# Staging the w3 columns of a two-layer spectral MLP kernel in a tile of their own

## The chip, the cores and the metric

The kernel runs on one core of one Trainium2 chip. The metric is device time in microseconds (us), the median over runs; lower is better. The core has a matrix engine (TensorE, PE in the profile), a vector engine (DVE), an activation engine (ACT), GpSimd (POOL) and SyncE (SP), whose queue here issues all the DMAs. Each engine works through its own list of instructions in program order, and semaphores tie the lists together.

## What is computed

Two layers, each made of a Fourier mixing block A and an MLP block B, over x of 2048 rows by 512 columns:

```python
# A: mixing
a = einsum("bsd,ed->bse", x, hid_re);  b = einsum("bsd,ed->bse", x, hid_im)
y = einsum("ts,bse->bte", seq_re, a) - einsum("ts,bse->bte", seq_im, b)
# B: spatial-shift mixing, then a channel MLP
h  = gelu(layernorm(x) @ w1)                 # four column groups shifted by +1, -1, +2, -2 rows
x1 = x + shifted(h) @ w2
B  = x1 + gelu(layernorm(x1) @ w3) @ w4      # w3: 512 x 1376, w4: 1376 x 512
# twice:
x = x + A(layernorm(x));  x = x + B(layernorm(x))
```

All is float32. The kernel gets the accuracy by splitting each operand into a high part (a cast to the matmul format, made on ACT) and a low part (operand minus high part, made on DVE), and by three matmuls for each product: high by high, high by low, low by high (`mm3`, lines 280 to 283).

## The kernel before

The rows are worked on in four chunks of 512. `by_pairs` (line 753) does block B. First it goes through w1 and w2 for all four chunks (`shifted` and `mixed`). Small jobs beside these products have written-down places: `D(slot, ...)` and `A(slot, ...)` put a job at slot 8c + 0..7 of chunk c, before (D) or after (A) the vector work of that slot. These jobs make, of chunks 0 and 1 (in layer 1 later also 2 and 3), the normalised input z3 of the second MLP. It goes through DRAM (`z3d`) to be turned, and comes back as blocks `b11`, `b21`, `b12`, `b22` and their Winograd sums `bt1` to `bt4`.

Then the product with w3 is done for two chunks at once, by a Winograd scheme of seven products instead of eight. Layer 1 does both pairs of chunks in this way, layer 0 one pair, and then chunks 2 and 3 by the plain `mlp` (line 699) with a stream of weights through `raw` and `ring`.

The loop over pairs of w3 column tiles (line 1048; p = 0 to 4) takes seven w3 units of one buffer `w3b[p % 2]`. Units 4, 5, 0 and 6 are tiles of w3 as they are; four sums (`w3_sums`, line 871) make units 0 to 3. In layer 0 the kernel makes highs (`w3_highs`), lows (`w3_lows`) and stores the whole 1792 KB buffer to DRAM (`w3_keep`, line 886), from where layer 1 loads it ready-made.

One turn of the loop has this order on PE, each `prod` being six matmuls:

```python
prod(b1, w, 4, "11"); copy u       # ACT takes b1 out of PSUM
prod(b6, w, 1, "t2"); v = u + b6   # add(): DVE, line 446
prod(b5, w, 0, "t1"); x = v + b5
prod(b2, w, 5, "21"); u = u + b2;  gelu and split of u
prod(b7, w, 2, "t3"); v = v + b7;  y = v + b5;  gelu of y
w4_part x 2                        # 12 matmuls each, of the turn before (one in turn 0)
prod(b4, w, 6, "t4"); v = v + b4;  gelu and split of v
prod(b3, w, 3, "22"); x = x + b3;  gelu of x
```

The seven results go round in four PSUM banks, so that a product begins only when the result four products earlier has been taken out.

In the kernel before, `w3_load(n)` puts the raw tiles of column pair n straight into the low half of `w3b[n % 2]` (lines 868 and 869). The loop issues it at the end of turn p for pair p + 2 (line 1092), when the buffer's last product has been issued. The sums, splits and stores for pair p + 1 and the same for two w4 tiles stand in a list `prep`; `one()` (line 997) takes the next entry from `prep`, or when it is empty from the background list `bg`. `bg` holds the z3 work of chunks 2 and 3 (`finish`: two sums each on DVE and the normalisation on ACT; `turn3`: transposes on DVE; `turn_out`: four stores of 256 KB).

`w4_load`, `w4_high` and `w4_low` (lines 838 to 855) do for tiles of w4 what the above does for w3: load, cast, low part and store to DRAM. There are six buffers `w4r`; each load waits until PE is done with its buffer. After the loop come two more `w4_part` for the pair's first chunk and eleven for the second, with one `one()` after each of the eleven. Then chunks 2 and 3 begin with `mlp`, whose first weight pieces are loaded by `more` (line 1104) and split by `ahead` from `bg`.

Of the kernel before, what the change touches and what calls it, by code (L numbers as in the profile page):

```python
# [19 lines left out]
CH = 512  # L20
# [13 lines left out]
RAW = 4  # L34
# [9 lines left out]
def spectral_mlp_kernel(ctx: ExitStack, tc: tile.TileContext, x, ws, hs, w1, w2, w34, out):  # L44
# [32 lines left out]
    base = -(-nc.sbuf_base // 32) * 32  # L77
    EXT = RNG + RING * 4 * CH
    RAWS = EXT + 6 * D
    nc.alloc_sbuf_tensor("arena", [P, RAWS + RAW * 2 * CH], F32)  # L80

    def at(name, word, *shape, dtype=F32R):
        return nc.alloc_sbuf_tensor_at(name, [P, *shape], dtype, offset=base + 4 * word).ap()
# [27 lines left out]
    w3b, w3bf = zip(*(both(f"w3b{i}", RNG + 8 * CH + i * 28 * P, 2, 7, 2 * P) for i in range(2)))  # L111
    h4 = [at(f"h4{i}", RR + 8 * CH + i * 2 * CH, 2, CH) for i in range(4)]
    hc = at("hc", W12, NF, CH, dtype=F32)
    w4_at = [ZW + i * 2 * CH for i in range(4)] + [W12 + NF * CH + i * 2 * CH for i in range(2)]
    w4r, w4rf = zip(*(both(f"w4r{i}", word, 2, CH) for i, word in enumerate(w4_at)))
    scratch = [at(f"scr{i}", RNG + w * 4 * CH, KD, CH, dtype=F32) for i, w in enumerate((2, 3, 0))]
# [636 lines left out]
    def by_pairs(layer, zs, xin, dst):  # L753
# [107 lines left out]
        def w3_load(n):  # L861
            if n >= n_pairs * (NF // 2):
                return
            if layer:
                nc.sync.dma_start(w3b[n % 2].bitcast(F32), w3d[n % (NF // 2)])
                return
            lo = w3bf[n % 2][:, 1]
            nc.sync.dma_start(lo[:, 4:6], w34[2 * n][:, 0].rearrange("p (u w) -> p u w", u=2))
            nc.sync.dma_start(lo[:, 0:7:6], w34[2 * n + 1][:, 0].rearrange("p (u w) -> p u w", u=2))

        def w3_sums(n):

            lo = w3bf[n % 2][:, 1]
            add(lo[:, 2], lo[:, 4], lo[:, 0], ALU.subtract)
            add(lo[:, 0], lo[:, 0], lo[:, 6])
            add(lo[:, 1], lo[:, 0], lo[:, 4], ALU.subtract)
            add(lo[:, 3], lo[:, 5], lo[:, 1], ALU.subtract)

        def w3_highs(n, a, b):
            nc.scalar.copy(w3b[n % 2][:, 0, a:b], w3bf[n % 2][:, 1, a:b])  # L880

        def w3_lows(n, a, b):
            w = w3b[n % 2]
            nc.vector.tensor_tensor(w[:, 1, a:b], w3bf[n % 2][:, 1, a:b], w[:, 0, a:b].bitcast(F32), op=ALU.subtract)  # L884

        def w3_keep(n):
            nc.sync.dma_start(w3d[n], w3b[n % 2].bitcast(F32))
# [75 lines left out]
        D(25, u_stats(2, 2))  # L963

        A(26, lambda: w3_load(0))
        A(28, lambda: w3_load(1), *[w4_load] * 4)
        if layer == 0:
            A(30, lambda: w4_high(0), lambda: w4_high(1))
            D(31, lambda: w4_low(0), lambda: w4_low(1), lambda: w3_sums(0))
            A(31, lambda: w3_highs(0, 0, 7))  # L970
        for c in range(NC):
            tmps[:] = extra[4:6]
            count["tmp"] = 0
# [18 lines left out]
            for q in range(TC):  # L992
                nc.vector.tensor_tensor(xt(c * TC + q), acc[q], xt(c * TC + q), op=ALU.add)

        bg, prep = [], []

        def one():
            if prep:
                prep.pop(0)()
            elif bg:  # L1000
                bg.pop(0)()

        for pair in range(n_pairs):
# [2 lines left out]
            acc2 = [bk[(1 + i) % 4] for i in range(4)]  # L1006
            if pair == 0:
                bg += [finish(2, 0), finish(2, 2), turn3(turned, 2, 0, 1), turn3(turned, 2, 2, 3)]
                bg += [lambda: turn_out(turned, z3d[2]), u_stats(3, 0), u_stats(3, 2), finish(3, 0), finish(3, 2)]
                bg += [turn3(turned, 3, 0, 1), turn3(turned, 3, 2, 3), lambda: turn_out(turned, z3d[3])]  # L1010
            tmps[:] = gs
            if layer == 0:
                w3_lows(0, 0, 4)
                w3_lows(0, 4, 7)
            s = w4_use()
            for i, names in enumerate((("11", "21"), ("12", "22"))):
                for d in range(KD):
# [13 lines left out]

            def w_prep(p):

                todo = []
                if p == 0:
                    todo.append(lambda: w3_keep(0))
                if p + 1 < NF // 2:
                    todo.append(lambda: (w3_sums(p + 1), w3_highs(p + 1, 0, 4)))
                    todo.append(lambda: (w4_high(2 * p + 2), w3_highs(p + 1, 4, 7)))
                    todo.append(lambda: (w3_lows(p + 1, 0, 4), w4_high(2 * p + 3)))  # L1040
                    todo.append(lambda: (w3_lows(p + 1, 4, 7), w3_keep(p + 1)))
                    todo.append(lambda: (w4_low(2 * p + 2), w4_low(2 * p + 3)))
                else:
                    todo.append(lambda: (w4_high(NF - 1), w4_high(NF)))
                    todo.append(lambda: (w4_low(NF - 1), w4_low(NF)))
                return todo

            for p in range(NF // 2):
                if layer == 0:
                    prep += w_prep(p)  # L1050
                u, v, x, y = sets[p % 2]
                w = w3b[(5 * pair + p) % 2]
                b1, b6, b5, b2, b7, b4, b3 = (bk[(2 + 7 * p + i) % 4] for i in range(7))
                prod(b1, w, 4, "11")
                nc.scalar.copy(u, b1)
                if layer == 0:
                    one()
                prod(b6, w, 1, "t2")
                add(v, u, b6)
                prod(b5, w, 0, "t1")  # L1060
                one()
                add(x, v, b5)
                prod(b2, w, 5, "21")
                add(u, u, b2)
                gelu_split(h4[2 * (p % 2)], u, act)
                if layer == 0:
                    one()
                prod(b7, w, 2, "t3")
                add(v, v, b7)
                add(y, v, b5)  # L1070
                gelu(hc[:, 2 * p + 1], y)
                one()
                if p == 0:
                    w4_part(acc1, fs[0], h4[2], None if layer else one)
                    w4_load()
                else:
                    for i in range(2):
                        w4_part(acc1, 2 * p - 2 + i, h4[2 * ((p - 1) % 2) + i], None if layer else one)
                        w4_load()
                        one()  # L1080
# [6 lines left out]
                if layer == 0:  # L1087
                    one()
                prod(b3, w, 3, "22")
                add(x, x, b3)  # L1090
                gelu(hc[:, 2 * p], x)
                w3_load(5 * pair + p + 2)
                one()

            if layer and pair == 0:
# [3 lines left out]
                bg += [sum_of("t1", "12", "11"), sum_of("t2", "22", "t1"), sum_of("t3", "22", "12"), sum_of("t4", "21", "t2")]  # L1099
                bg += [parts(b) for b in ("11", "21", "12", "22", "t2", "t1", "t3", "t4")]  # L1100
            if layer == 0:
                nothing = lambda: None

                def more():
                    state.update(limit=w_items[1], load=len(pieces))
                    issue_dma()

                bg += [nothing, lambda: rt_in(2), more, nothing, nothing]
                bg += [lambda: rt_split(2, ((0, 2),)), lambda: rt_split(2, ((2, 4),)), lambda: ahead(1), lambda: ahead(1), lambda: ahead(1)]
            for i in range(2):  # L1110
                w4_part(acc1, NF - 3 + i, h4[i])
                w4_load()
# [12 lines left out]
            if last:  # L1125
                ss = [w4_use(), w4_use()]
                for q in range(TC):
                    v = slice(q * P, (q + 1) * P)
                    for k, s in zip((NF - 2, NF - 1), ss):
                        h = h4[(2 + k) % 4]  # L1130
                        mm3(acc2[q], h[:, 0, v], h[:, 1, v], s[:, 0], s[:, 1], False, k == NF - 1)
                    j = c2 * TC + q
                    nc.vector.tensor_tensor(xt(j), acc2[q], xt(j), op=ALU.add)
                    rows(xs[j // 2][:, j % 2 : j % 2 + 1], dst, j, 1, False)
            else:
                drain(c2, acc2)
                for j in range(c2 * TC, c2 * TC + TC, 2):
                    rows(xs[j // 2], dst, j, 2, False)
                while bg or prep:
                    one()  # L1140

    for layer in range(LAYERS):
# [148 lines left out]
        tmps[:] = singles  # L1291
        for c in (2, 3):
            for t in mlp(c, acc4, mm4):
                if c == 2 and t == 0:
                    rt_in(3)
                if c == 2 and t in (9, 10):
                    rt_split(3, ((2 * t - 18, 2 * t - 16),))
                if c == 3 and t == 1:
                    for j in range(2 * TC, 3 * TC, 2):
                        rows(xs[j // 2], x2d, j, 2, False)  # L1300
                n = STEPS * (c - 2) + t - 6
                if n >= 0:
                    if n == 0:
                        tmps[:] = [tmp[:, 4], tmp[:, 5]]
                    for k in range(6):
                        for step, f in enumerate(xp_stages):
                            if n == FIRST[k] + step:
                                f(k)
# [55 lines left out]
```

## Time and profile before

| | |
|---|---|
| runs | 1497.39, 1495.9, 1496.81 us; median 1496.81 |
| the profiled execution | 1495.02 us, of which 1493.2 us are the span from the first to the last instruction |
| busy share of the span | PE 98%, DVE 75%, ACT 48%, POOL 6% |
| DMA | 277.17 MB, mean 186 GB/s; HBM read 231.21 MB, written 44.83 MB |
| mean granted TensorE clock | 0.994 |

A row of a profile names the line of the kernel, the engine, the operation, and the tiles as output<-inputs, with buffer numbers left out: `rest` are the tiles u, v, x and y of the loop, `psa` and `psd` PSUM banks, `in_w` the raw weights in DRAM. In a row of a timeline the first number is the start in us, the second the duration, and what stands in brackets at the end is the idle time of the engine just before and who ended it. SPq is the DMA queue of SP: its row tells when a DMA is issued and how long issuing takes, and a separate row "DMA to landing" how long it takes from issue until the data have landed. A row of waits gives who waited at which line for whom, the sum in us, how often, and the longest. Matmuls overlap: one lasts about 0.39 us and the next begins after some 0.23.

### The profile page before, as it was taken

The numbers are of one execution on the slowest core, as the hardware profiler recorded it, in microseconds if no ns is written. First come the engines' busy times: TensorE is split into PE (matmuls) and PEld (weight loads), VectorE is DVE, ScalarE is ACT, GpSimd is POOL, SyncE is SP. The second block draws the span as 40 slices with busy tenths as digits, with TensorE's granted clock in tenths as the row PEclk, the third lists the DMA queues.
The fourth block names the chain that finished last, engine by engine and source line by source line (L and its number), as shares of the span: only waits on it lengthen the run. The fifth ranks groups of instructions, "written<-read, shape, count | busy, mean of one in ns | idle before, by whom it ended". The sixth has DMA issues, their size and how long they took to land.

```text
span 1493.2 us, 17313 instructions
## 1 busy us (share of the span) xinstructions
PE 1461.2 (98%) x6374; PEld 1193.8 (80%) x6374; DVE 1122.5 (75%) x1553; ACT 713.9 (48%) x947; POOL 85.6 (6%) x111
## 2 busy tenths in 40 slices
PE   9999999999999977999999999999999999999998
PEld 7888888888878755788787888888888888888887
DVE  6876987988778865555989889979978688646443
ACT  5563454544566633333646444544545566333231
POOL 2100000000001000000100000000000010000000
PEclk9999999999999999999999999999999999999999
DMA  6326556566446554761434566455575358668434
GB/s 232 135 90 207 197 184 223 172 206 243 158 131 183 194 207 159 270 232 62 140 134 156 172 209 204 163 199 209 165 257 184 127 152 299 198 217 309 157 134 155
DMA packets 111220, 277.17 MB, mean 186 GB/s; under 512 B 8480, under 2 KB 38432, under 8 KB 109216
## 3 DMA queue, kind: packets, MB, share of 16 engines
q1 hardware_dynamic: 111136, 276.07, 55.0%
q8 instruction: 50, 0.82, 0.2%
q14 instruction: 34, 0.28, 0.1%
HBM read 231.21 MB, written 44.83 MB: 185 GB/s over the span
## 4 chain that ended last, share of the span: by engine, by line
PE 81%; DVE 11%; DMA 3%; ACT 2%; issue 1%; SPq 1%; POOL 0%; DVEq 0%; ACTq 0%
PE psd L281 9%; PE psd L283 9%; PE psd L282 9%; PE psa L281 7%; PE psa L283 7%; PE psa L282 7%; PE psc L283 6%; PE psc L281 6%; PE psc L282 6%; PE psb L283 5%; PE psb L281 5%; PE psb L282 5%; DVE ring L244 3%; DMA raw<-in_ws 2%; DVE w3b L884 1%
## 5 line engine op out<-in xcount | busy, mean ns | idle before, releaser
L228 ACT CAST ring<-raw 128x1024 fp32r<-128x1024 f32 (+1 forms) x153 | 156.2, 1029 | 117.9 <-PE psd L283 49.3
L244 DVE TENSOR_TENSOR ring<-raw,ring 128x1024 fp32r<-128x1024 f32 (+1 forms) x153 | 181.6, 1191 | 27.9 <-ACT ring L228 27.5
L282 PE MATMUL psd<-ring,rr 128*128 128x512 f32 x208 | 80.9, 389 | 0.0
L281 PE MATMUL psd<-ring,rr 128*128 128x512 f32 x208 | 80.9, 389 | 0.0
L283 PE MATMUL psd<-ring,rr 128*128 128x512 f32 x208 | 80.9, 389 | 0.0
L645 DVE TENSOR_TENSOR h<-tmp,h 128x512 fp32r<-128x512 f32 x53 | 36.7, 692 | 49.4 <-ACT h L644 47.6
L321 POOL TENSOR_TENSOR rs<-ve,mhalf 128x4 f32<-128x4 f32 x16 | 27.8, 1738 | 611.7 <-DVE nm L320 611.7
L300 POOL TENSOR_TENSOR rs<-ve,mhalf 128x2 f32<-128x2 f32 (+1 forms) x33 | 32.8, 993 | 448.6 <-DVE nb L299 439.0
L329 ACT ACTIVATE tmp<-xs,nb,rs 128x512 f32<-128x512 f32 x58 | 44.7, 808 | 18.7 <-POOL nb L301 18.7
L235 ACT CAST ring<-ring2f 128x1024 fp32r<-128x1024 f32 x28 | 29.6, 1057 | 43.5 <-DVE ring2f L234 43.5
L281 PE MATMUL psc<-ring,ay 128*128 128x512 f32 x128 | 49.9, 390 | 0.3 <-ACT rr11f L471 0.3
L282 PE MATMUL psc<-ring,ay 128*128 128x512 f32 x128 | 49.9, 390 | 0.2 <-DVE ring L244 0.2
L283 PE MATMUL psc<-ring,ay 128*128 128x512 f32 x128 | 49.8, 389 | 0.0
L281 PE MATMUL psb<-ring,ay 128*128 128x512 f32 x128 | 49.8, 389 | 0.0
L282 PE MATMUL psb<-ring,ay 128*128 128x512 f32 x128 | 49.8, 389 | 0.0
L283 PE MATMUL psb<-ring,ay 128*128 128x512 f32 x128 | 49.8, 389 | 0.0
L244 DVE TENSOR_TENSOR ring<-ring1f,ring 128x1024 fp32r<-128x1024 f32 (+1 forms) x50 | 49.1, 983 | 0.5 <-ACT ring L235 0.3
L244 DVE TENSOR_TENSOR ring<-ring3f,ring 128x1024 fp32r<-128x1024 f32 (+1 forms) x50 | 49.1, 983 | 0.2
L235 ACT CAST ring<-ring0f 128x1024 fp32r<-128x1024 f32 x28 | 29.6, 1057 | 41.1 <-DVE ring0f L234 41.1
L282 PE MATMUL psa<-ring,ay 128*128 128x512 f32 x126 | 49.0, 389 | 0.0
L283 PE MATMUL psa<-ring,ay 128*128 128x512 f32 x126 | 49.0, 389 | 0.0
L281 PE MATMUL psa<-ring,ay 128*128 128x512 f32 x126 | 49.0, 389 | 0.0
(474 smaller groups left out, 4377.2 us busy)
## 6 DMA issues: line engine op xcount, KB each, us to landing
raw<-in_ws SPq DMA_DIRECT2D x183, 512.0 KB, 4.8
raw<-in_hs SPq DMA_DIRECT2D x56, 512.0 KB, 3.5
w4r<-w4d SPq DMA_DIRECT2D x55, 512.0 KB, 3.7
w3b<-w3d SPq DMA_DIRECT2D x10, 1792.0 KB, 7.2
raw<-in_w SPq DMA_DIRECT2D x26, 512.0 KB, 3.6
w3d<-w3b SPq DMA_DIRECT2D x5, 1792.0 KB, 5.7
x1d<-tmp SPq DMA_DIRECT2D x12, 512.0 KB, 6.8
xs<-x1d SPq DMA_DIRECT2D x12, 512.0 KB, 6.6
```

The lines of the kernel that those rows point to most:

```text
L228: nc.scalar.copy(dest[:, a:b, 0], r[0][:, a:b])
L235: nc.scalar.copy(dest[:, :, 0], lo)
L244: nc.vector.tensor_tensor(lo, src, hi.bitcast(F32), op=ALU.subtract)
L281: nc.tensor.matmul(o, lh, rh, start=first, stop=False)
L282: nc.tensor.matmul(o, lh, rl, start=False, stop=False)
L283: nc.tensor.matmul(o, ll, rh, start=False, stop=last)
L300: nc.gpsimd.tensor_tensor(rs[:, :n], ve[:, :n], mhalf[:, 0, :n], op=ALU.pow)
L321: nc.gpsimd.tensor_tensor(rs, ve, mhalf[:, :, :2], op=ALU.pow)
L329: nc.scalar.activation(o, s, AF.Identity, bias=mr[2], scale=mr[1])
L645: nc.vector.tensor_tensor(dst[:, 1], g, dst[:, 0].bitcast(F32), op=ALU.subtract)
L884: nc.vector.tensor_tensor(w[:, 1, a:b], w3bf[n % 2][:, 1, a:b], w[:, 0, a:b].bitcast(F32), op=ALU.subtract)
```

## The change

- A new tile `staged` (1024 words per partition) lies behind the arena; the DMA scratch, which nothing in the kernel uses, gets smaller in its place.
- In layer 0 `w3_load(n)` loads both raw tiles of column pair n into `staged` by one DMA. `w3_sums`, `w3_highs` and `w3_lows` read units 4, 5 and 6 from there, and write the buffer `w3b` only with results. Highs and lows come in up to three pieces: the sums (units 0 to 3), units 4 and 5, unit 6.
- The load of pair n + 1 is issued right behind the store of pair n, when the lows of pair n have read `staged`. Pair 0 is loaded where it was, pair 1 behind the first store.
- The list `prep` becomes a table of fixed points: after the first product (0), before the sum of the third (1), after the fourth (2), after the fifth (3), in the middle of the first `w4_part` (4) and of the second (5).
- Ahead of the loop, part of pair 0's splits and its sums move to slots 29 to 31, and the lows of the first two w4 tiles move from slot 31 to behind the last sum of `mixed`.
- In layer 0 the z3 work of chunk 3 moves from the loop to the background jobs behind it (with a scratch tile in place of the part of `hc`), ahead of `more`; `rt_in(2)` comes right behind the loop, `rt_in(3)` one step later in `mlp`.
- In layer 1, turn 0 has one `one()` more, and the second `w3_load` stands behind four `w4_load`.

```diff
-            lo = w3bf[n % 2][:, 1]
-            nc.sync.dma_start(lo[:, 4:6], w34[2 * n][:, 0].rearrange("p (u w) -> p u w", u=2))
-            nc.sync.dma_start(lo[:, 0:7:6], w34[2 * n + 1][:, 0].rearrange("p (u w) -> p u w", u=2))
+            nc.sync.dma_start(staged.rearrange("p f k w -> p f (k w)"), w34[2 * n : 2 * n + 2, :, 0].rearrange("f p w -> p f w"))
...
+        def w3_sums(n, half):
+            lo, (a, b) = w3bf[n % 2][:, 1], (staged[:, i] for i in range(2))
+            if half == 0:
+                add(lo[:, 2], a[:, 0], b[:, 0], ALU.subtract)
+                add(lo[:, 0], b[:, 0], b[:, 1])
+            else:
+                add(lo[:, 1], lo[:, 0], a[:, 0], ALU.subtract)
+                add(lo[:, 3], a[:, 1], lo[:, 1], ALU.subtract)
+
+        def w3_of(n):
+            return (slice(0, 4), w3bf[n % 2][:, 1, 0:4]), (slice(4, 6), staged[:, 0]), (slice(6, 7), staged[:, 1, 1:2])
...
-        A(28, lambda: w3_load(1), *[w4_load] * 4)
+        A(28, *[w4_load] * 4)
         if layer == 0:
+            A(29, lambda: w3_highs(0, 1, 2))
+            D(30, lambda: w3_lows(0, 1, 2), lambda: w3_sums(0, 0))
             A(30, lambda: w4_high(0), lambda: w4_high(1))
-            D(31, lambda: w4_low(0), lambda: w4_low(1), lambda: w3_sums(0))
-            A(31, lambda: w3_highs(0, 0, 7))
+            D(31, lambda: w3_sums(0, 1))
+            A(31, lambda: w3_highs(0, 0))
+        else:
+            A(28, lambda: w3_load(1))
...
             if layer == 0:
-                w3_lows(0, 0, 4)
-                w3_lows(0, 4, 7)
+                w4_low(0)
+                w4_low(1)
+                w3_lows(0, 0)
+                w3_keep(0)
+                w3_load(1)
...
+                n, i = p + 1, 2 * p + 2
...
+                return {
+                    0: [lambda: w3_sums(n, 0), lambda: w3_highs(n, 1, 2)],
+                    1: [lambda: w3_sums(n, 1), lambda: w3_highs(n, 0)],
+                    2: [w4_highs],
+                    3: [lambda: w3_lows(n, 0)],
+                    4: [lambda: w3_lows(n, 1, 2), lambda: w3_keep(n), lambda: w3_load(n + 1)],
+                    5: [w4_lows],
+                }
...
-                w3_load(5 * pair + p + 2)
+                if layer:
+                    w3_load(5 * pair + p + 2)
...
-                bg += [nothing, lambda: rt_in(2), more, nothing, nothing]
-                bg += [lambda: rt_split(2, ((0, 2),)), lambda: rt_split(2, ((2, 4),)), lambda: ahead(1), lambda: ahead(1), lambda: ahead(1)]
+                rt_in(2)
+                bg += z3_last(scratch[0])
+                bg += [lambda: (more(), rt_split(2, ((0, 2),))), lambda: rt_split(2, ((2, 4),)), *[lambda: ahead(1)] * 3]
```

`z3_last(t)` is the list of chunk 3's jobs: two `u_stats`, two `finish`, one `turn3`, and a second `turn3` with the `turn_out`.

More of the change, by code (lines that the diff above doesn't have):

```diff
@@ L79, in spectral_mlp_kernel @@
     RAWS = EXT + 6 * D
-    nc.alloc_sbuf_tensor("arena", [P, RAWS + RAW * 2 * CH], F32)
+    STG = RAWS + RAW * 2 * CH
+    nc.alloc_sbuf_tensor("arena", [P, STG + 2 * CH], F32)
     def at(name, word, *shape, dtype=F32R):
@@ L113, in spectral_mlp_kernel @@
     hc = at("hc", W12, NF, CH, dtype=F32)
+    staged = at("staged", STG, 2, 2, 2 * P, dtype=F32)
     w4_at = [ZW + i * 2 * CH for i in range(4)] + [W12 + NF * CH + i * 2 * CH for i in range(2)]
@@ L866, in w3_load, with w3_highs, w3_lows @@
                 return
-            lo = w3bf[n % 2][:, 1]
[L868 to L882, printed above, removed]
+            nc.sync.dma_start(staged.rearrange("p f k w -> p f (k w)"), w34[2 * n : 2 * n + 2, :, 0].rearrange("f p w -> p f w"))
[9 more added lines that the diff above has]
+            return (slice(0, 4), w3bf[n % 2][:, 1, 0:4]), (slice(4, 6), staged[:, 0]), (slice(6, 7), staged[:, 1, 1:2])
+        def w3_highs(n, *which):
+            for i in which:
+                units, src = w3_of(n)[i]
+                nc.scalar.copy(w3b[n % 2][:, 0, units], src)
+        def w3_lows(n, *which):
             w = w3b[n % 2]
-            nc.vector.tensor_tensor(w[:, 1, a:b], w3bf[n % 2][:, 1, a:b], w[:, 0, a:b].bitcast(F32), op=ALU.subtract)
+            for i in which:
+                units, src = w3_of(n)[i]
+                nc.vector.tensor_tensor(w[:, 1, units], src, w[:, 0, units].bitcast(F32), op=ALU.subtract)
         def w3_keep(n):
@@ L993, in drain, with at_point @@
                 nc.vector.tensor_tensor(xt(c * TC + q), acc[q], xt(c * TC + q), op=ALU.add)
-        bg, prep = [], []
+        bg, prep = [], {}
+        def at_point(i):
+            for f in prep.pop(i, ()):
+                f()
         def one():
-            if prep:
-                prep.pop(0)()
-            elif bg:
+            if bg:
                 bg.pop(0)()
@@ L1008, in by_pairs @@
                 bg += [finish(2, 0), finish(2, 2), turn3(turned, 2, 0, 1), turn3(turned, 2, 2, 3)]
-                bg += [lambda: turn_out(turned, z3d[2]), u_stats(3, 0), u_stats(3, 2), finish(3, 0), finish(3, 2)]
-                bg += [turn3(turned, 3, 0, 1), turn3(turned, 3, 2, 3), lambda: turn_out(turned, z3d[3])]
+                bg += [lambda: turn_out(turned, z3d[2])]
+                z3_last = lambda t: [
+                    *(u_stats(3, 0), u_stats(3, 2), finish(3, 0), finish(3, 2)),
+                    *(turn3(t, 3, 0, 1), lambda: (turn3(t, 3, 2, 3)(), turn_out(t, z3d[3]))),
+                ]
+                if layer:
+                    bg += z3_last(turned)
             tmps[:] = gs
             if layer == 0:
-                w3_lows(0, 0, 4)
-                w3_lows(0, 4, 7)
+                w4_low(0)
[3 more added lines that the diff above has]
+                w3_load(1)
             s = w4_use()
@@ L1032, in w_prep @@
             def w_prep(p):
[L1034 to L1046, printed above, removed]
+                n, i = p + 1, 2 * p + 2
+                w4_lows = lambda: (w4_low(i), w4_low(i + 1))
+                w4_highs = lambda: (w4_high(i), w4_high(i + 1))
+                if n == NF // 2:
+                    return {1: [w4_highs], 5: [w4_lows]}
+                return {
[6 more added lines that the diff above has]
+                }
             for p in range(NF // 2):
-                if layer == 0:
-                    prep += w_prep(p)
+                prep = {} if layer else w_prep(p)
                 u, v, x, y = sets[p % 2]
@@ L1055, in by_pairs @@
                 nc.scalar.copy(u, b1)
-                if layer == 0:
-                    one()
+                at_point(0)
                 prod(b6, w, 1, "t2")
@@ L1060, in by_pairs @@
                 prod(b5, w, 0, "t1")
-                one()
+                if layer:
+                    one()
+                at_point(1)
                 add(x, v, b5)
@@ L1065, in by_pairs @@
                 gelu_split(h4[2 * (p % 2)], u, act)
-                if layer == 0:
-                    one()
+                at_point(2)
                 prod(b7, w, 2, "t3")
@@ L1071, in by_pairs @@
                 gelu(hc[:, 2 * p + 1], y)
-                one()
-                if p == 0:
-                    w4_part(acc1, fs[0], h4[2], None if layer else one)
-                    w4_load()
[L1076 to L1080, printed above, removed]
+                if layer:
+                    one()
+                at_point(3)
+                tiles = [(fs[0], h4[2])] if p == 0 else [(2 * p - 2 + i, h4[2 * ((p - 1) % 2) + i]) for i in range(2)]
+                for i, (f, h) in enumerate(tiles):
+                    w4_part(acc1, f, h, lambda: at_point(4 + i))
+                    w4_load()
+                    one()
+                at_point(4)
+                at_point(5)
                 if p == NF // 2 - 1:
@@ L1086, in by_pairs @@
                 gelu_split(h4[2 * (p % 2) + 1], v, act)
-                if layer == 0:
-                    one()
                 prod(b3, w, 3, "22")
@@ L1091, in by_pairs @@
                 gelu(hc[:, 2 * p], x)
-                w3_load(5 * pair + p + 2)
+                if layer:
+                    w3_load(5 * pair + p + 2)
                 one()
@@ L1101, in by_pairs @@
             if layer == 0:
-                nothing = lambda: None
                 def more():
@@ L1138, in by_pairs @@
                     rows(xs[j // 2], dst, j, 2, False)
-                while bg or prep:
+                while bg:
                     one()
@@ L1293, in spectral_mlp_kernel @@
             for t in mlp(c, acc4, mm4):
-                if c == 2 and t == 0:
+                if c == 2 and t == 1:
                     rt_in(3)
@@ L1352 @@
     arrays = {f"in_{k}": np.ascontiguousarray(v) for k, v in arrays.items()}
-    nc = bacc.Bacc("TRN2", target_bir_lowering=False, num_devices=1, dynamic_dma_scratch_size=1024)
+    nc = bacc.Bacc("TRN2", target_bir_lowering=False, num_devices=1, dynamic_dma_scratch_size=512)
     args = [
```

## Prediction

> **What bounds the kernel now.** I read the page first, then TensorE's waits, then the stage in which they lie, cut into the five turns of its loop, and last the queues of that stage in order of time.
>
> ```profile
> span 1493.2 us, 17313 instructions
> ```
> ```profile
> PE psa L281 <- DVE rest L446: 11.8, 5, 4.5
> PE psd L281 <- DVE rest L446: 8.9, 6, 3.2
> ```
>
> The columns are us in total, times, and the longest. TensorE (PE) waits little in the whole span, and nearly all of it (20.7 us) is for line 446, the vector sums that empty its banks. All eleven waits lie in layer 0's loop over pairs of w3 columns. Busy time by turn (p = 0 to 4; each ends where the next one's first product begins):
>
> ```profile
> 511.41:526.20 14.79, 13.12 (x55) 9.91 (x54) 10.97 (x19) 8.58 (x13) 0.00 (x0) 1.00 0.36 143
> 526.20:549.06 22.86, 17.57 (x67) 12.99 (x66) 14.36 (x24) 6.96 (x11) 0.00 (x0) 0.92 0.47 181
> 549.06:575.82 26.76, 18.84 (x67) 14.04 (x66) 16.33 (x34) 8.49 (x14) 2.04 (x4) 0.88 0.57 187
> 575.82:601.54 25.72, 18.44 (x67) 13.47 (x66) 13.71 (x23) 8.47 (x13) 0.00 (x0) 0.90 0.54 185
> 601.54:617.54 16.00, 16.00 (x68) 13.01 (x67) 8.82 (x14) 6.85 (x12) 0.00 (x0) 0.94 0.97 348
> ```
>
> After the length come PE, weight loads, DVE, ACT, POOL (busy us and count), then granted clock, DMA share and GB/s. A turn has 42 products of w3 and 24 of w4 (12 in the first), 318 in all. An undisturbed stretch of layer 1 gives the pace:
>
> ```profile
> 1178.00:1242.00 64.00, 64.00 (x283) 51.89 (x282) 52.39 (x106) 41.03 (x60) 9.54 (x16) 1.00 0.59 175
> ```
>
> About 281 of these 283 start inside, so 0.2276 us each: 66 take 15.0 us, 318 take 72.4. The loop takes 106.1, so 33.7 us are lost there, 2.3% of the span. No engine is full in turns 1 to 3 (DVE 14.36 of 22.86); it is a chain of waits. What starts it:
>
> ```profile
> DVE w3b0f L446 <- DMA w3b0f<-in_w: 14.2, 2, 8.8
> DVE w3b1f L446 <- DMA w3b1f<-in_w: 7.1, 1, 7.1
> ```
>
> DVE stands before its sums of w3 tiles until they have landed, 21.3 us in three waits, and behind it in its queue stand the sums that free PE's banks. The tiles are late because of where SyncE (SP) issues them:
>
> ```profile
> 547.22 0.33 SPq L887 DMA_DIRECT2D w3d<-w3b  x1
> 547.78 1.47 SPq L855 DMA_DIRECT2D w4d<-w4r  x2
> 549.37 1.16 SPq L844 DMA_DIRECT2D w4r2f<-in_w  x1
> 550.58 6.57 SPq L595 DMA_DIRECT2D z3d<-hc  x4
> 557.26 1.84 SPq L844 DMA_DIRECT2D w4r3f<-in_w  x1
> 559.20 1.40 SPq L868 DMA_DIRECT2D w3b1f<-in_w  x1
> 560.65 0.47 SPq L869 DMA_DIRECT2D w3b1f<-in_w  x1
> ```
> ```profile
> 564.54 1.80 DVE L446 TENSOR_TENSOR w3b1f<-w3b1f 128x256 f32<-128x256 f32 x4 [7.06 <-DMA w3b1f<-in_w]
> ```
>
> The load of column pair 3 comes last in that list, behind four stores of z3; DVE's sums follow its landing at once.
>
> **The change, part by part.**
>
> *The loop.* The load for n+1 now goes to its own tile right behind the store w3_keep(n), as soon as DVE has run the last lows of n. It no longer waits for PE or stands behind z3's stores. But there is one staging tile, so a circle remains: landing, DVE's work to the lows, store and load, landing. If it is longer than PE's 15.0 us it sets the turn. Its durations, from starts that follow each other without a gap:
>
> ```profile
> 503.71 0.68 DVE L686 TENSOR_TENSOR rest<-psd,rest 128x512 f32<-128x512 f32 x1
> 504.31 1.21 DVE L407 TENSOR_TENSOR bt<-bt4f,bt 128x1024 fp32r<-128x1024 f32 x1
> 505.45 0.68 DVE L854 TENSOR_TENSOR w4r<-w4r0f,w4r 128x512 fp32r<-128x512 f32 x1
> 506.05 0.68 DVE L854 TENSOR_TENSOR w4r<-w4r1f,w4r 128x512 fp32r<-128x512 f32 x1
> 506.65 1.79 DVE L446 TENSOR_TENSOR w3b0f<-w3b0f 128x256 f32<-128x256 f32 x4
> 508.36 0.68 DVE L686 TENSOR_TENSOR rest<-psa,rest 128x512 f32<-128x512 f32 x1
> ```
> ```profile
> 528.73 0.69 DVE L645 TENSOR_TENSOR h<-tmp,h 128x512 fp32r<-128x512 f32 x1 [1.35 <-ACT h L644]
> 531.14 1.30 DVE L573 STREAM_TRANSPOSE hc<-tmp 128x512 f32<-128x512 f32 x2
> ```
>
> An instruction of 512 columns costs 0.60, of 1024 columns 1.14, four of 256 columns 1.71 (0.43 each), and a gelu with its cast on ACT makes DVE idle 1.35. DVE's order in a turn from the landing on: two sums 0.86, v 0.60, two sums 0.86, x and u 1.20, the idle 1.35, the split's low 0.60, v and y 1.20, then w3's lows of 4, 2 and 1 units 1.14 + 0.60 + 0.43. Sum 8.8, and 9.0 with the handovers. ACT's highs (three instead of two) lie beside it; each runs while DVE is at x and u.
>
> The rest of the circle is the transfer. For the store at 547.22, and the two stores of 512 KB issued behind it, the times from issue to landing are:
>
> ```profile
> DMA to landing us min/median/max: 5.7/5.7/5.7
> ```
> ```profile
> DMA to landing us min/median/max: 6.5/7.1/7.8
> ```
>
> The 1792 KB landed at 552.9; the first store behind it, issued at 547.78, landed after 6.5, at 554.3. So 512 KB behind it cost 1.4, and the staged load should land 7.1 after the store's issue, 7.3 after the lows. The nearest other rows bound it: 5.7, if it does not queue, and the longest that 512 KB took in this stage (two loads of w4r at 602):
>
> ```profile
> DMA to landing us min/median/max: 9.8/10.2/10.5
> ```
>
> ```profile
> 600.21 0.33 SPq L887 DMA_DIRECT2D w3d<-w3b  x1
> 600.77 1.49 SPq L855 DMA_DIRECT2D w4d<-w4r  x2
> 602.35 2.48 SPq L846 DMA_DIRECT2D w4r<-w4d  x2
> ```
>
> Those two had the 1792 KB and two stores of 512 KB just ahead; the staged load has the 1792 KB alone. So I take 7.3. The circle is 9.0 + 7.3 = 16.3 us, 1.3 over PE's 15.0: the loop stays bound by this chain, but at 16.3 instead of 25. DVE then comes to the wait 4.4 us after the lows (two w4 lows 1.20, v 0.60, idle 1.35, low 0.60, x 0.60) and stands some 2.9 us. Queued behind that stand are the bank sums of the turn, for which PE waits, and on ACT, whose highs wait for the same tile, the turn's gelus.
>
> *The start.* Here the change costs. DVE's rows from 503.71 to 508.36 leave no gap, and the low of the first w4 tile at 505.45 is what PE needs:
>
> ```profile
> 506.18 0.50 PE L283 MATMUL psd<-b,w4r 128*128 128x512 f32 x1
> ```
>
> This third matmul began at the low's end (506.13). Now before that low come w3's lows of 2 and 1 units (1.03), all four sums (1.71) and the last sum of line 686 (0.60): 3.34 us later, at 509.47. PE stands 3.3 us, and its first product of w3 moves from 511.41 to 514.75. Behind the two w4 lows come w3's lows of 4 units, done at 511.2, then store and load. The first store of before found a loaded queue:
>
> ```profile
> DMA to landing us min/median/max: 8.1/8.1/8.1
> ```
>
> Two stores of 512 KB will stand ahead here too, so 8.1 and 1.4 behind 511.3: the second pair's tiles land at 520.8.
>
> *The sum on the trace's clock.* Landings at 520.8, 537.1, 553.4 and 569.7. The last gets 1.0 more: z3's chunk 2 still goes out in turn 1 behind the third load, and from 547.22 to 564.54 the same transfers kept the queue busy 17.3 us, against 16.3 to the next store. So 570.7; lows done 579.7; two w4 lows 580.9; v 581.5; gelu and cast 582.9; the low 583.5; x 584.1. That x frees the bank for turn 4's fourth product, and 48 matmuls are left: 10.9 us, the loop ends at 595.1. Before it ended at 617.54: 22.4 us less, start included.
>
> *PE's clock.* The 3.3 us gap at the start may lower the clock:
>
> ```profile
> 593.23 0.79 PE L281 MATMUL psd<-bt,w3b 128*128 128x512 f32 x1 [2.63 <-DVE rest L446]
> 593.82 0.63 PE L282 MATMUL psd<-bt,w3b 128*128 128x512 f32 x1
> 594.25 0.63 PE L283 MATMUL psd<-bt,w3b 128*128 128x512 f32 x1
> ...
> 599.33 0.50 PE L281 MATMUL psd<-b,w3b 128*128 128x512 f32 x1 [3.17 <-DVE rest L446]
> ```
>
> After a gap of 2.63 us matmuls came every 0.43, 0.20 over the pace. Turn 3's granted clock of 0.90 is, at half speed, 2 x 0.10 x 25.72 = 5.1 us slow; as it had these two gaps, one costs 2.6 us of it, six matmuls, 1.2 us. In my sum that is hidden: in turn 0 PE waits for the landing anyway. By the Trainium skill ("TensorE: Matmul & The Clock Gate", HAM oscillation) only idle gaps over about 3.4 us matter, so this gap would cost nothing; the trace speaks against that, since 2.63 sufficed. By either the sum stays, as the cover is there; without it the price is 0 or 1.2.
>
> *Behind the loop.* The rest of z3's chunk 3 (two statistics, four sums, four transposes, about 8 us of DVE) moves out of the loop to the following stretch, and four stores of 256 KB and then the first loads of the next stage's weight stream follow it on SP:
>
> ```profile
> 617.54:655.00 37.46, 37.46 (x164) 30.49 (x163) 17.68 (x24) 11.76 (x18) 0.00 (x0) 1.00 0.71 255
> ```
>
> DVE has 19.8 idle there, so it fits. But order matters: the transposes end after the fifth w4 tile, 84 matmuls (19.1), a cast and low (1.9) and 1.2: 22.2 us behind the loop's end. Four stores issue in up to 6.6 (the z3d row above), then the streamed tile; with the longest landing, 10.5, and 1.2 for its split it is ready at 40.5. PE needs it after 156 matmuls, at 35.5. Bounds 0 and 5.0; I take 0.2, since the queue is emptier here than for the 10.5. The rest costs 0: chunk 3's load one step later, a background slot more in layer 1, the smaller scratch, and in layer 1 the second w3 load behind four w4 loads: 4 x 1.4 = 5.6 later, hidden by the 126 matmuls (28.7) ahead of its first use; without that cover, 5.6.
>
> Sum: -22.4 + 0.2 = -22.2. The profiled run took 1495.02 (span plus 1.8), 1.8 under the median 1496.81; I carry the difference over: 1474.6.
>
> **The rivals.**
> - *The loads vanish wholly.* If the landing is within 6.0 of the lows, PE sets the pace: 514.75 + 72.4 = 587.2, 30.3 less: 1466.5 (1467.7 with the slow matmuls). For: the store alone lands in 5.7. Against: the load is behind it. Chance 0.15.
> - *The landing is long*, 10.5 as in the row: 3.2 more at each of four landings, 12.8: 1487.4. For: in turn 1 z3's and w4's stores follow the load and may share the engines with it. Against: only the store is queued ahead. Chance 0.14.
> - *The tail takes some back*, 5.0 us: 1479.6. Chance 0.06.
> - *Slower:* the single tile ties each load to DVE's lows, and DVE's bank sums to the load. Four landings have to give back 22.2, 5.6 each: from a landing of 12.9 us on the kernel is slower; at 14.5 it is 6.6 us slower, 1503.4. Against: no row of the stage is over 10.5. Chance 0.03.
> - *It doesn't do what it says*: the load still lands as late, and the turns stay at 25. Against: SP's queue has nothing that waits between lows and load. Chance 0.02.
>
> **How the numbers follow.** My forecast, 0.60: 1474.6. The range is 1467 to 1484: down to the loads vanishing, up to a landing of 9.6 (2.35 more, four times); half of the first rival, most of the second's upper end and the last two are left out. No change is within 0.2%, about 3 us, which measurements of this kernel can just tell. Faster 0.95, same 0.02, slower 0.03.
>
> **What would show it.** Right: turns of 16 to 17 us; DVE's longest wait for the staged tile 2 to 4 us, PE's longest in the loop under 2; the third matmul of w4r waiting some 3 us for line 854's successor; the loop ending 22 us earlier; no PE wait where the streamed stage begins. Wrong: turns of 15 (the circle is shorter), waits of DVE for DMA that stay over 6, or a PE wait behind the loop over 2.

## The result and the profile after

| | before | changed |
|---|---|---|
| median of the runs, us | 1496.55 | 1480.74 |
| lowest and highest | 1495.9 to 1497.39 | 1479.5 to 1482.24 |
| profiled execution, us | 1495.02 | 1479.5 |
| its span | 1493.2 | 1477.6 |
| from the first w3 product in layer 0 to the end of its loop | 106.1 | 82.4 |

The ratio is 0.9894, with a 95% interval of 0.9877 to 0.9912: the change takes 15.8 us off, where 22.2 were forecast. One run of a kernel tried below, the store in halves, took 2441.76 us at a granted clock of 0.556 and is left out of that kernel's figures. The five turns of the loop in the changed kernel (length, then PE, weight loads, DVE, ACT, POOL, granted clock, DMA share, GB/s):

```profile
516.85:529.20 12.35, 12.35 (x56) 10.14 (x54) 9.20 (x16) 8.25 (x14) 0.00 (x0) 1.00 0.19 65
529.20:546.64 17.44, 15.77 (x68) 12.15 (x67) 11.98 (x21) 7.28 (x12) 0.00 (x0) 1.00 0.60 211
546.64:564.57 17.93, 15.62 (x67) 12.15 (x66) 10.63 (x19) 7.27 (x12) 0.00 (x0) 1.00 0.84 279
564.57:582.89 18.32, 15.80 (x67) 12.15 (x66) 10.64 (x19) 7.26 (x12) 0.00 (x0) 1.00 0.60 215
582.89:599.22 16.33, 15.48 (x68) 12.24 (x66) 10.95 (x18) 6.86 (x12) 0.00 (x0) 1.00 0.91 330
```

Turns 1 to 3 take 17.4 to 18.3 us instead of 22.9 to 26.8, and the clock is no longer lowered in them. But they do not take PE's 15.0 either. The waits in this stretch say why. Each row gives who waited for whom, total us, times, longest:

```profile
DVE w3b0f L448 <- DMA staged<-in_w: 6.7, 2, 4.5
...
DVE w3b1f L448 <- DMA staged<-in_w: 5.5, 2, 4.1
...
PE psa L283 <- DVE rest L448: 3.8, 4, 1.5
...
PE psd L283 <- DVE rest L448: 3.5, 3, 1.7
PE psd L285 <- DVE w4r L856: 3.2, 1, 3.2
```

DVE still stands before every landing, 12.2 us in four waits instead of 21.3 in three. PE's waits for the bank sums (line 448 now) fell from 20.7 to 7.3 us, all of them under 1.8, and a new one of 3.2 us for the first w4 low has come. What one turn of the circle is made of is seen in DVE's rows (start, length, idle before):

```profile
555.82 0.76 DVE L448 TENSOR_TENSOR w3b1f<-staged 128x256 f32<-128x256 f32 x2 [4.10 <-DMA staged<-in_w]
...
564.19 1.03 DVE L893 TENSOR_TENSOR w3b<-staged,w3b 128x512 fp32r<-128x512 f32 x2
...
574.14 0.76 DVE L448 TENSOR_TENSOR w3b0f<-staged 128x256 f32<-128x256 f32 x2 [4.48 <-DMA staged<-in_w]
```

From the landing at 555.8 to the end of the last lows at 565.2 are 9.4 us, from there to the next landing 8.9. Between them DVE's second pair of sums stands 0.4 for ACT's highs:

```profile
557.58 0.43 DVE L448 TENSOR_TENSOR w3b1f<-w3b1f,staged 128x256 f32<-128x256 f32 x1 [0.40 <-ACT w3b L887]
```

SP's queue shows the store and the load right behind each other:

```profile
565.30 0.32 SPq L896 DMA_DIRECT2D w3d<-w3b  x1
565.67 0.43 SPq L869 DMA_DIRECT2D staged<-in_w  x1
566.22 0.88 SPq L846 DMA_DIRECT2D w4r4f<-in_w  x1
567.19 2.53 SPq L857 DMA_DIRECT2D w4d<-w4r  x2
```

The times from issue to landing, of that store and of that load:

```profile
DMA to landing us min/median/max: 6.8/6.8/6.8
```
```profile
DMA to landing us min/median/max: 8.4/8.4/8.4
```

The store lands later than the 5.7 of before, and the load 8.7 behind the store's issue, where the prediction had 7.1.

### The profile page after: what moved, and what is told of

Same layout as the page of the kernel before. It is cut to its first block, busy times and chain, and to the rows that moved or that the text cites. A ratio compares the mean times of both kernels' runs of the same rounds, so it can differ in the third digit from the quotient of the medians.

```text
span 1477.6 us, 17320 instructions
## 1 busy us (share of the span) xinstructions
PE 1455.5 (99%) x6374; PEld 1190.9 (81%) x6374; DVE 1121.9 (76%) x1558; ACT 715.5 (48%) x953; POOL 86.8 (6%) x111
## 4 chain that ended last, share of the span: by engine, by line
PE 80%; DVE 11%; DMA 4%; ACT 2%; issue 2%; SPq 0%; POOL 0%; DVEq 0%; ACTq 0%
PE psd L285 9%; PE psd L283 8%; PE psd L284 8%; PE psa L283 7%; PE psa L285 7%; PE psa L284 7%; PE psc L285 6%; PE psc L283 6%; PE psc L284 6%; PE psb L285 6%; PE psb L283 6%; PE psb L284 6%; DVE ring L246 2%; DMA raw<-in_ws 2%; DMA staged<-in_w 1%
## 5 line engine op out<-in xcount | busy, mean ns | idle before, releaser
L283 PE MATMUL psc<-ring,ay 128*128 128x512 f32 x128 | 49.9, 390 | 0.3 <-ACT rr11f L473 0.3
L284 PE MATMUL psb<-ring,ay 128*128 128x512 f32 x128 | 49.9, 390 | 0.2 <-DVE ring L246 0.2
L285 PE MATMUL psa<-ring,ay 128*128 128x512 f32 x126 | 49.0, 389 | 0.0
L283 PE MATMUL psd<-ring,ay 128*128 128x512 f32 x126 | 49.0, 389 | 0.0
L284 PE MATMUL psa<-ring,ay 128*128 128x512 f32 x126 | 49.0, 389 | 0.0
```

The lines of the kernel that those rows point to most:

```text
L283: nc.tensor.matmul(o, lh, rh, start=first, stop=False)
L284: nc.tensor.matmul(o, lh, rl, start=False, stop=False)
L285: nc.tensor.matmul(o, ll, rh, start=False, stop=last)
```

## The experiments

Each kernel was timed against the kernel before in runs on the same chip; the table gives its median and ratio with the 95% interval (the kernel with w4 lows later has one run alone, and so no ratio).

| kernel | us | ratio | loop, us | TensorE's first w3 product |
|---|---|---|---|---|
| the change | 1480.74 | 0.9894 (0.9877 to 0.9912) | 82.4 | 516.85 |
| the change, again | 1479.74 | 0.9889 (0.9873 to 0.9905) | 84.5 | 516.14 |
| load ahead of the store | 1470.12 | 0.9827 (0.9813 to 0.9840) | 74.6 | 516.45 |
| w4 lows back | 1480.25 | 0.9895 (0.9882 to 0.9909) | 90.0 | 510.92 |
| both | 1465.45 | 0.9799 (0.9785 to 0.9812) | 76.2 | 511.20 |
| both, again | 1466.66 | 0.9797 (0.9783 to 0.9811) | 76.2 | 510.43 |
| z3 back in the loop | 1482.54 | 0.9911 (0.9898 to 0.9925) | 89.5 | 514.26 |
| w4 lows later | 1489.31 | | 94.7 | 514.32 |
| store in halves | 1468.34 | 0.9817 (0.9801 to 0.9834) | 74.5 | 515.86 |
| both, short lows first | 1467.71 | 0.9811 (0.9796 to 0.9825) | 76.1 | 511.38 |
| load at its old place | 1494.66 | 0.9994 (0.9984 to 1.0003) | 97.8 | 517.18 |
| halves and w4 lows back | 1466.96 | 0.9805 (0.9791 to 0.9819) | 77.5 | 511.12 |

The loop is counted from the start of the first w3 product to the start of the last w3 matmul plus 0.23. The theory was that a circle sets the turn: the landing of the staged tile, DVE's work down to the lows that free it, store and load, the next landing.

**The order of store and load.**

```diff
-                w3_keep(0)
                 w3_load(1)
+                w3_keep(0)
...
-                    4: [lambda: w3_lows(n, 1, 2), lambda: w3_keep(n), lambda: w3_load(n + 1)],
+                    4: [lambda: w3_lows(n, 1, 2), lambda: w3_load(n + 1), lambda: w3_keep(n)],
```

> The changed kernel with one order reversed: the load of the next staged pair is issued ahead of the 1792 KB store instead of behind it. Theory A (the loop is bound by a circle: landing, 9.4 us of DVE work to the lows, store and load, landing 8.6 us later): the load no longer stands behind the store and lands some 3 to 4 us after its issue, the circle falls to about 13 us, under TensorE's 15.0 per turn, and the loop takes 72.4 us at TensorE's pace plus at most 1, instead of 82.4: about 9.5 us less than the changed kernel, near 1471. Theory B (the landing is long because of what the stage moves in all, not because of the order): the landing stays over 7 us, turns stay near 18, no difference above 2 us. Theory C (DVE, not the landing, sets the turn): no difference either, but the landing comes early and DVE no longer stands before it.

It took 1470.12. SP now issues the two in this order, and from issue to landing the four loads took:

```profile
545.10 0.38 SPq L869 DMA_DIRECT2D staged<-in_w  x1
545.58 0.41 SPq L896 DMA_DIRECT2D w3d<-w3b  x1
```
```profile
DMA to landing us min/median/max: 4.4/5.0/6.5
```

The loop came to 74.6, against 72.4 at TensorE's pace and the 73.4 that theory A allowed; nearly all that is over lies in turn 1, which took 17.0. What is left of the waits in the loop is:

```profile
DVE w3b0f L448 <- DMA staged<-in_w: 2.2, 1, 2.2
...
PE psd L283 <- DVE rest L448: 1.0, 1, 1.0
...
PE psa L283 <- DVE rest L448: 0.3, 1, 0.3
```

One swap of two lines in SP's queue, with the same bytes and the same work, is worth 10.6 us by the medians, 9.6 against the second set of runs of the changed kernel. That speaks for A and against B and C. The landing was longer than A had it: 4.4 to 6.5 us, not 3 to 4. With 4.4 to 4.5, in turns 1 and 2, it is short enough, as 15.0 less 9.4 is 5.6. The last one, 6.5 with three other transfers still under way, is not: before it DVE stands the 2.2 us shown, but TensorE had no wait from that.

**The start.**

```diff
-            D(30, lambda: w3_lows(0, 1, 2), lambda: w3_sums(0, 0))
...
-            D(31, lambda: w3_sums(0, 1))
+            D(31, lambda: w4_low(0), lambda: w4_low(1), lambda: w3_lows(0, 1, 2), lambda: w3_sums(0, 0), lambda: w3_sums(0, 1))
...
-                w4_low(0)
-                w4_low(1)
                 w3_lows(0, 0)
```

> The changed kernel with the start undone: the first two w4 lows go back ahead of the moved lows and sums of w3 (slot 31), so the first product waits as little as before the change. TensorE's first w3 product then begins some 5.8 us earlier (511 instead of 516.85). Theory A (from the second landing on the circle sets the time, and the store of pair 0 is issued no earlier): the landing of the second pair stays at about 519.4 and the total changes by less than 1 us. Theory D (the start adds to the total in full, 3.2 us of waiting and 2.6 us of half clock): 5.8 us less, near 1475.

TensorE began its w3 products 5.9 us earlier and the kernel took the same time, 1480.25. The time gained at the start is stood out in turn 0:

```profile
520.71 0.76 DVE L448 TENSOR_TENSOR w3b1f<-staged 128x256 f32<-128x256 f32 x2 [6.39 <-DMA staged<-in_w]
```

DVE stands 6.4 us before the second pair's landing, which comes at 520.7 instead of 519.4, not earlier. So the start's cost was hidden behind the circle, as theory A and the prediction had it.

> Both edits together. If the reversed order leaves the loop at TensorE's pace (theory A), the start is no longer covered by the circle, and what the second edit was worth nothing for alone it is worth here: 5.8 us on top of the first edit, about 15 us less than the changed kernel, near 1465.5. If the first edit does nothing (B or C), this comes out as the second alone.

With the reversed order the cover is gone, and the same edit brings 4.7 us by the medians (3.5 by the second set of runs, 1466.66), where 5.8 were expected: 1465.45, the lowest median of the study, 2.0% under the kernel before. The first w3 product begins 5.3 us earlier, and the loop ends 3.7 earlier (587.36 for 591.01), since it is 1.6 longer. What an edit is worth depends on what ends last beside it: nothing with the circle, some 4 us without.

**The z3 work.**

```diff
-                    *(u_stats(3, 0), u_stats(3, 2), finish(3, 0), finish(3, 2)),
+                    *(lambda: (u_stats(3, 0)(), u_stats(3, 2)()), lambda: (finish(3, 0)(), finish(3, 2)())),
...
-                if layer:
-                    bg += z3_last(turned)
+                bg += z3_last(turned)
...
-                bg += z3_last(scratch[0])
```

> The changed kernel with the z3 work of chunk 3 put back into the loop (with its jobs in fewer, larger pieces, so that its scratch tiles are free again in time). Theory A: DVE stands 2 to 4.5 us before each landing, so its some 8 us in turns 1 and 2 fill those waits; four more stores of 256 KB lengthen one landing by 1 to 3 us: 0 to 4 us slower than the changed kernel. Theory C (DVE sets the turn): 7 to 8 us slower.

1482.54: 1.8 us slower than the change, though its loop is 7.1 us longer. Of that, 2.6 are an earlier start (514.26), so the loop ends 4.6 later (603.77 for 599.22; 3.1 later than in the changed kernel's second profile, 600.63). Nothing comes back behind the loop: the 1600 matmuls from its end on take 365.7 us in both. The medians need not differ as these profiles do, as executions also differ further behind (see below). Against the changed kernel, 1.8 lies within A's 0 to 4 and below C's 7 to 8: moving z3 out is worth little while the circle sets the time.

**What lengthens the landing.** Two kernels ask why it is 8.1 to 8.6 us.

```diff
...
-                    2: [w4_highs],
+                    2: ([lambda: (w4_low(i - 2), w4_low(i - 1))] if p else []) + [w4_highs],
...
-                    5: [w4_lows],
```

> The changed kernel with the lows of the two w4 tiles, and so their two stores of 512 KB, moved from right behind w3's lows to the fourth product of the next turn (behind the landing). It asks why the staged load lands 8.1 to 8.6 us after its issue and not the 6.7 to 7.1 that the row of before promised. Theory S (the load and the store share the DMA engines, what follows is not the cause): the landing stays at 8 to 8.6. Theory F (the w4 stores that follow within 1.5 us take part of the engines' time): it falls to 7.2 or less. The two w4 lows now lie inside the circle and add 1.2 us to DVE's part in turns 1 to 3, so the time itself says little: 1480 to 1484.

Without the w4 stores behind it, the load landed in turns 1 to 3 in 7.7 to 8.0, between theory S (8 or more) and theory F (7.2 or less). It is 0.7 to 0.8 less in the two turns in which the w4 stores had followed closely, and 0.1 less in the one in which z3's stores stand between. Most of the length stays. But what follows a load can cost more than that, as the first load of the same kernel shows. Here the gap at the start left the clock up, so PE was done with a w4 tile earlier and the next w4 load (line 846) was issued 3.3 us behind the staged load, not 6.0 as in the changed kernel:

```profile
511.18 0.68 SPq L869 DMA_DIRECT2D staged<-in_w  x1
514.51 0.33 SPq L846 DMA_DIRECT2D w4r0f<-in_w  x1
```
```profile
DMA to landing us min/median/max: 10.1/10.1/10.1
```

In the changed kernel that landing took 8.3; with the w4 load 4.9 behind, in its second profile, 8.9; and again 3.3 behind, with z3 back in the loop, 10.2. So theory F has a part. Why the w4 load costs more here than in the later turns, where it follows 0.5 behind, stays open. The time was a miss, 1489.31, since w4 lows stood in DVE's queue behind the landing, and PE's w4 products waited for them:

```profile
PE psc L284 <- DVE w4r L856: 13.1, 4, 6.9
```

The fixed point 5, straight behind the w3 lows, is thus a place that matters.

```diff
-            nc.sync.dma_start(w3d[n], w3b[n % 2].bitcast(F32))
+            nc.sync.dma_start(w3d[n][:, 0], w3b[n % 2][:, 0].bitcast(F32))
+
+        def w3_keep_low(n):
+            nc.sync.dma_start(w3d[n][:, 1], w3b[n % 2][:, 1].bitcast(F32))
...
+                w3_keep_low(0)
...
-                    4: [lambda: w3_lows(n, 1, 2), lambda: w3_keep(n), lambda: w3_load(n + 1)],
+                    4: [lambda: w3_lows(n, 1, 2), lambda: w3_keep(n), lambda: w3_load(n + 1), lambda: w3_keep_low(n)],
```

> The changed kernel with the store of a w3 buffer in two halves of 896 KB, and the staged load between them. Halfway between the changed kernel (1792 KB ahead, landing 8.6) and the reversed order (nothing ahead, 4.4 to 7.6). Theory A (what is ahead in the queue sets the landing): landing some 6 to 6.5, circle 15.5 to 16, 5 to 7 us less than the changed kernel, near 1475. Theory S (store and load share the engines whatever their order by less than a microsecond): landing over 7.5, at most 3 us less.

1468.34, a larger gain than expected. SP's rows tell why this kernel is not the halfway case in the middle of the loop:

```profile
538.84 0.32 SPq L896 DMA_DIRECT2D w3d<-w3b  x1
544.46 0.38 SPq L869 DMA_DIRECT2D staged<-in_w  x1
544.89 0.46 SPq L899 DMA_DIRECT2D w3d<-w3b  x1
```

A store of the high half waits only for ACT's highs, so it leaves 5.6 us ahead of the load and has landed (3.5 us) before it. The load has nothing in front and lands in 4.3; so it is with the load before it (4.5). For the first load the half store is issued just 0.6 ahead, and that is the halfway case: it landed in 7.1, where it took 8.3 with the whole store ahead and 5.6 with none (the load ahead of the store). That fits theory A. The last load, with the half store 2.8 ahead and z3's and w4's transfers around it, took 6.2.

**The load earlier still.**

```diff
-                    3: [lambda: w3_lows(n, 0)],
-                    4: [lambda: w3_lows(n, 1, 2), lambda: w3_load(n + 1), lambda: w3_keep(n)],
+                    3: [lambda: w3_lows(n, 1, 2), lambda: w3_load(n + 1)],
+                    4: [lambda: w3_lows(n, 0), lambda: w3_keep(n)],
```

(against the kernel with both edits)

> The kernel with both edits (load ahead of the store, w4 lows at their old place) and, besides, w3's short lows and the load one point earlier, ahead of the long low. The load is issued some 1.1 us earlier. In the kernel with both edits DVE stood before the landing 2.3 us in all and TensorE 2.3 us in the loop; at most these go: 0 to 1.5 us less than 1465.5. If the loop is already at TensorE's pace, no difference above 0.5.

1467.71: no gain, the loop is as long as with both edits (76.1 for 76.2), though the load lands in 3.5 to 3.6 in turns 0 and 1. From turn 2 on the loop is at TensorE's pace (15.0 to 15.1 a turn) in both; the difference to 1465.45 lies within the intervals of the two ratios.

**The load at its old place.**

```diff
-                    4: [lambda: w3_lows(n, 1, 2), lambda: w3_keep(n), lambda: w3_load(n + 1)],
+                    4: [lambda: w3_lows(n, 1, 2), lambda: w3_keep(n)],
...
-                if layer:
-                    w3_load(5 * pair + p + 2)
+                w3_load(5 * pair + p + 2)
```

> The changed kernel with one part undone: the staged load goes back to the end of the turn (its old place), behind the w4 stores and loads on SP's queue; staging tile and fixed points stay. Theory A (place in the queue, not the tile of its own, makes the gain): the load is issued some 5 us later and behind 1 MB more, the circle grows from 18 to about 21, three times 3 us: about 9 us slower than the changed kernel, near 1489. Theory E (the tile of its own, which frees the load from TensorE's last product, is what counts): within 2 us of the changed kernel.

1494.66, no faster than the kernel before that can be told. The direction is theory A's, the size is larger: 14 us, not 9. The load is issued in turn 1 behind the stores of z3 and w4, and these take SP longer than I had counted:

```profile
550.70 6.45 SPq L597 DMA_DIRECT2D z3d<-hc  x4
557.24 3.45 SPq L857 DMA_DIRECT2D w4d<-w4r  x2
560.80 1.01 SPq L846 DMA_DIRECT2D w4r3f<-in_w  x1
561.86 1.13 SPq L869 DMA_DIRECT2D staged<-in_w  x1
```

It is issued 12 us behind the store of 549.85 instead of 0.4, and DVE stands 13.4 us before that landing. Staging tile and fixed points are all still there. The loop is 8.3 us shorter than before the change (97.8 for 106.1), but begins 5.8 later, so with the load at this place they bring nothing that shows in the time; the place in SP's queue does.

**Behind the loop.** In the changed kernel's profile the loop ended 18.3 us earlier (599.22 against 617.54), but the span is only 15.6 shorter. Of these 2.7 us, 2.5 went in layer 1's mixing, whose code is the same; between 1080 and 1140 us TensorE waited there:

```profile
PE psc L285 <- DVE rr L409: 1.4, 1, 1.4
PE psc L284 <- DVE ring L246: 1.2, 1, 1.2
PE psb L284 <- DVE ring L246: 0.2, 1, 0.2
```

> The changed kernel itself once more, beside the two best versions. Its profile had lost 2.7 us behind the loop, in layer 1's mixing, where the code is untouched; five of nine profiles of its relatives lost 1 to 3 us there and the others nothing. Theory P (belongs to the kernel, as where its transfers fall in time): a second profile shows the same loss of 2.7 within 0.5. Theory R (differs from run to run): it shows another loss or none. Time 1480.7 within 1.

> The kernel with both edits (load ahead of the store, w4 lows at their old place) once more: it had lost nothing in layer 1's mixing. Theory P: again nothing. Theory R: it may lose. Time 1465.5 within 1.

The kernel before has one wait there, of 0.9. The changed kernel's second profile (1479.74 median) lost less than 0.1 there, with one wait of 0.9, and the second profile of both edits (1466.66) lost 2.4, where its first had lost 0.1. So it differs from run to run, theory R; it belongs to no kernel, and it sets how closely single profiles can be compared. Why these waits come in some executions and not in others wasn't tried.

> The store in two halves with the load between them, and the w4 lows at their old place. The store in halves alone ended its loop 0.6 us earlier than the load ahead of the whole store; with the start uncovered the second edit should be worth some 4.7 us here too: 1464.5 to 1465.5, the same as both edits within 1 us. If the half store's gain had come from a better start, it is less.

1466.96, 0.3 us over both edits in the same runs, which the intervals can't tell apart: no better than the simpler swap. The second edit was worth 1.4 us here by the medians and 1.8 by the ratios, not 4.7. TensorE's first w3 product came 4.7 earlier than with halves alone, but the loop is 3.0 longer, and DVE stands before the first landing in it:

```profile
517.09 0.76 DVE L448 TENSOR_TENSOR w3b1f<-staged 128x256 f32<-128x256 f32 x2 [2.57 <-DMA staged<-in_w]
```

With both edits that tile landed at 513.9. Here the first load stands behind a half store again, so the landing still covers part of what is gained at the start.

## Why the prediction was right, and where its size was off

*What bounds the loop.* Right: DVE stood before the tiles, and the loads were late by their place in SP's queue. The load at its old place shows it, by giving the gain back.

*The circle.* Right as a mechanism (order reversed, start undone). Its size was off, and this is the step that failed: "So I take 7.3". From the lows to the landing it took 8.5 to 9.1. The row behind the 7.3 was a store behind a store; the change puts a load behind it. The store itself then lands in 6.7 to 7.1 instead of 5.7, and the load 1.4 to 2.3 after it: each lands later for the other, where I had the load follow a store that it does not delay. DVE's part was 9.4, not 9.0; 0.4 is a wait of the second sums for ACT's highs, which I had put wholly beside DVE's work. The three circles took 17.9 to 18.5, 54.7 in all, where the forecast had 49.9 (three of 16.3, and 1.0 for z3's stores): 4.8 more. The first landing came 1.4 earlier than forecast (519.4), so the last was at 574.1 instead of 570.7, and from there the end took 0.7 longer. The loop's end at 599.2 is 4.1 later than forecast. That the first landing came near was in part luck: the two stores of 512 KB that were to stand ahead "too" had landed at 510.4 in the kernel before, ahead of the 8.1 us store's issue at 512.49, and with only a 256 KB load under way its length stays unexplained.

*The start.* The gap was 3.17 us for 3.3 forecast. The clock fell behind it, and for longer than I had priced: 13 matmuls 0.43 apart (508.97 to 514.68) cost 2.6, not 1.2.

```profile
508.97 0.80 PE L285 MATMUL psd<-b,w4r 128*128 128x512 f32 x1 [3.17 <-DVE w4r L856]
509.56 0.63 PE L283 MATMUL psd<-b,w4r 128*128 128x512 f32 x1
...
514.25 0.63 PE L285 MATMUL psd<-b,w4r 128*128 128x512 f32 x1
514.68 0.47 PE L283 MATMUL psd<-b,w4r 128*128 128x512 f32 x1
```

That it is hidden held: undoing the start alone brought nothing.

*Behind the loop.* The forecast was 0.2 and PE has no wait where the streamed stage begins; the tail rival is out. In the profiled execution 15.6 of the 22.2 us came: of the 6.6 missing, 4.1 are the loop's end, and 2.7 came behind it, nearly all in the mixing, where 0.2 were forecast for the tail. In the second profile the loop ended 5.5 later than forecast, and the mixing lost nothing to speak of.

*The rivals.* "The landing is long" came nearest: not 10.5, but half the way there. "The loads vanish wholly" describes the reversed order, with the moved start: 1470.12, the loop ending at 591.0, where that rival had 1466.5 and 587.2. That both edits come to 1465.45, near its figure, is chance, as their loop begins 3.6 earlier than the rival's and is 3.8 longer.

*The signs.* The first w4 wait (3.17), PE's longest wait in the loop after it (1.67, under 2) and the streamed stage without a wait came as named. Turns of 16 to 17 (17.4 to 18.3), a longest DVE wait of 2 to 4 (4.5) and a loop ending 22 us earlier (18.3) did not, and all three by the same longer circle.

## What to carry to other kernels

Here the staging tile brought no time until its load had the right place: look at which wait the load stands behind in its queue, and put a small load that is on the path ahead of a large store that is not. With one buffer, add up the circle (landing, work to its last reader, queue, landing) and compare it with the bound engine's turn; while it was longer here, another saving was worth nothing, and most of it came back when the circle was shortened. Price a transfer by a row of the same kind: a load behind a store is not a store behind a store.

## What the runs showed of the hardware

- From the loop's second store on, a 1792 KB store landed 5.7 us after its issue with 512 KB stores behind it, 6.3 to 6.4 with a 256 KB load issued 0.4 behind it, and 6.6 to 7.1 with a 512 KB load there. With nothing else under way ahead of it, a 512 KB load ahead of such a store took 4.3 to 4.5 with the store 0.4 to 0.5 behind it, 3.5 to 3.6 with the store 1.3 behind it. So loads and stores of one queue overlap in both orders, and each lands later for the other. The loop's first store took 8.1 in the kernel before, with no transfer behind it for 14 us; why stays open. The Trainium skill ("DMA: Bandwidth & Descriptors", Queues, rings and completion order) says that a DMA engine consumes descriptors in ring order while a later one may finish its write first. The landings agree that the order is no barrier, as a store lands later for a load behind it; that a later transfer lands first, no run here shows.
- The same gap of 3.1 to 3.2 us at the start had the first w3 product begin 5.2 us behind the gap's end in two kernels, as at full clock, and 6.5 to 7.9 behind it in five: what a gap costs in lowered clock differs by up to 2.7 us. The Trainium skill's figure of 3.4 us ("TensorE: Matmul & The Clock Gate", HAM oscillation) is no lower bound for it: 3.17 us had the clock down here.
